# Sums of weight blocks on one engine, and gates' steps at another place, in a fused scan and router kernel

## The chip, the cores and the metric

The kernel runs on one core of a Trainium2 chip. The metric is device time in microseconds: the median of several executions on the same chip. Five engines work from queues of their own, each in order: TensorE (PE, with PEld for its weight loads), VectorE (DVE), ScalarE (ACT), GpSimd (POOL) and SyncE (SP, which here only starts transfers). They wait for each other through semaphores.

## The reference

Two parts follow each other. First a state-space scan over 4 batches, 8 heads and 768 positions gives 3072 rows of 256 numbers. Then a router with 8 experts picks one expert for each row by cosine similarity, and the row goes through that expert's two layers:

```python
xn = x / (np.linalg.norm(x, axis=-1, keepdims=True) + 1e-06)
logits = xn @ en.T / tau
expert_idx = np.argmax(logits, axis=1)
probs = softmax(logits)                      # written out in the reference
gate_w = probs[np.arange(N), expert_idx]
for e in range(E):
    mask = expert_idx == e
    h = np.maximum(x[mask] @ w1[e], 0.0)     # 256 -> 1024
    out[mask] = gate_w[mask, None] * (h @ w2[e])   # 1024 -> 256
```

Everything is float32. The change touches only the second part.

## The kernel before

The scan (`mamba`, `scan_end`) takes the first part of the span, and overlaps the first two experts. Its rows, with the router's logits beside them, go to DRAM. A table of row numbers by expert is built on the way. Then each expert is a `Job`: GpSimd gathers its rows (up to 416, four blocks of 104) with indirect DMAs (`load`, L876), PE turns them (`turn_x`, L970), the first layer gives hT (1024 hidden values by 416 rows), the second layer gives yT (256 by 416), PE turns that back (`out`, L1182), ACT scales it by the gate (L1185), and GpSimd scatters the rows to the output with an indirect DMA (L1188). What exceeds the 416 rows of an expert is handled after the experts in a loop (`leftover`) that runs over no block for this data; its small tables are made by the generator `leftover_blocks`, a few VectorE instructions at each `next(left)`.

Experts 0 and 1 are done in halves with plain products. For experts 2 to 7, the layers' products are made with seven block products in place of eight (Winograd's form of Strassen's method): each matrix is cut in 2 x 2 blocks, and sums and differences of blocks stand in for some blocks.

- `sum_w1(which, engine)` (L1019) makes four sums S1[0] to S1[3] of blocks of w1, each 128 x 512, at L1026. `sum_w2(n)` (L1028) makes one of four sums S of blocks of w2, also 128 x 512, at L1034. S1[1] uses S1[0], and S1[3] uses S1[1]; the same holds for S.
- `sum_x` (T1, 128 x 208 each) and `sum_h` (T, 128 x 832 each) make the four differences of the rows' side, on VectorE, at L1038.
- `up_blocks` (L1056) is the first layer as a generator of 14 blocks of two matmuls each. Blocks 0, 1 use a block of w1 alone and ACT copies their result as `p1` (L1081); 2, 3 lead to a sum into hT on VectorE (L1090) and a relu on ACT (L1086); 4, 5 use S1[1] and are copied as `u2`; 6, 7 use S1[0]; 8, 9 use S1[2], are copied as `u3` and lead to the next hT sums; 10, 11 add to the bank that `u3` was copied from; 12, 13 use S1[3] and add to the bank that the hT sums of 8, 9 read.
- `down_blocks` (L1131) is the second layer: seven products of four matmuls, with six VectorE sums of 128 x 208 (L1148, `u2`, `v`, `u3` and three into yT). It yields after the first and after the second product group, and then runs to its end.
- `Gates` (L1197) makes the gate of each row: `square` (ACT, L1209), `power` (GpSimd, L1215: the square root), `largest` (VectorE, L1222 and L1224), `scale` (VectorE, L1230 to L1232), `exp` (ACT, L1237), `end` (VectorE, L1242 to L1244).

PSUM banks rotate: four named `yp`, three `hp`, one `ot`. Weights have three buffers of each kind, and SP loads those of expert i + 3 at the end of expert i's second layer, held behind the gates' power. The order of all instructions on each engine is written by hand in `moe` (L1248): the code inside the loop over `j.up_blocks()` runs after each of its 14 blocks, and so do the steps between the parts of `down_blocks`. In `moe`, expert i's first layer carries, on GpSimd, the four sums of its w2 (after blocks 0, 2, 4 and 6), the four scatters of the expert before (blocks 1, 3, 5, 7), and, on VectorE, S1[2] and S1[3] (block 3) and the gates' steps (blocks 4 to 6) with leftover steps (5 to 7). Its second layer carries, on GpSimd, the gathers for an expert further on, S1[0] and S1[1] of the next expert, and the power.

Of the kernel before, what the change touches and what calls it, by code (L numbers as in the profile page):

```python
# [22 lines left out]
DM, E, F = NH * D, 8, 1024  # L23
# [47 lines left out]
def hold(k, dma, after):  # L71

    k.tc.add_manual_dep(
        dma.ins, after.ins.name, mybir.DependencyInfo(mybir.DependencyClass.Sync, mybir.DependencyReason.SCHED_ONLY),
        reason="behind other transfers",
    )


def load_weights(k, e, parts=(0, 1), after=None):
    nc = k.nc  # L80
    if 0 in parts:
        k.w1t[e] = k.wp.tile([128, KD, F], F32, name="w1", tag="w1")
        for v in range(2):
            d = nc.sync.dma_start(
                k.w1t[e][64 * v : 64 * v + 64], k.w1[e].rearrange("(v z p) f -> v p z f", v=2, z=KD)[v]
            )
            if after is not None:
                hold(k, d, after)
    if 1 in parts:
        k.w2t[e] = k.wp.tile([128, KF, DM], F32, name="w2", tag="w2")  # L90
        d = nc.sync.dma_start(k.w2t[e][:], k.w2[e].rearrange("(f p) m -> p f m", p=128))
        if after is not None and 0 not in parts:
            hold(k, d, after)
# [845 lines left out]
class Job:  # L939
# [76 lines left out]
            (S[2], a[0][0], a[1][0], ALU.subtract), (S[3], a[0][1], S[1], ALU.subtract),  # L1016
        )

    def sum_w1(s, which, engine):  # L1019
        if 0 in which:  # L1020
            s.S1 = s.tile([128, 4, F // 2], "S1", 1)
        a = [[s.w1[:, j, F // 2 * i : F // 2 * i + F // 2] for j in range(2)] for i in range(2)]
        sums = s.sums_of([s.S1[:, n] for n in range(4)], a)
        for n in which:
            out, x, y, op = sums[n]
            engine.tensor_tensor(out=out, in0=x, in1=y, op=op)  # L1026

    def sum_w2(s, n):  # L1028
        if n == 0:
            s.S = s.tile([128, 4, KF // 2, 128], "S", 1)  # L1030
        w = s.w2
        a = [[w[:, 4 * j : 4 * j + 4, 128 * i : 128 * i + 128] for j in range(2)] for i in range(2)]
        out, x, y, op = s.sums_of([s.S[:, n] for n in range(4)], a)[n]
        s.k.nc.gpsimd.tensor_tensor(out=out, in0=x, in1=y, op=op)  # L1034

    def sum_inputs(s, T, b):
        for n, x, y in ((0, b[0][1], b[0][0]), (1, b[1][1], T[0]), (2, b[1][1], b[0][1]), (3, b[1][0], T[1])):
# [93 lines left out]
    def down_blocks(s):  # L1131


        k, nc, m = s.k, s.k.nc, s.nt * s.tr // 2
        s.yT = s.tile([128, KD, 2 * m], "yoT")
        w = [[s.w2[:, 4 * j : 4 * j + 4, 128 * i : 128 * i + 128] for j in range(2)] for i in range(2)]

        def product(t, a, b, start=True):
            for f in range(4):
                nc.tensor.matmul(  # L1140
                    t, lhsT=a[:, f], rhs=b[:, f], start=start and f == 0, stop=(f == 3), skip_group_check=True
                )

        def bank():
            return s.bank("yp", 4)[:, 0:m]

        def add(out, x, y):
            nc.vector.tensor_tensor(out=out, in0=x, in1=y, op=ALU.add)  # L1148

        def part(name):  # L1150
            return s.tile([128, m], name, 1)[:]

        p1, u2, u3, v = (part(n) for n in ("q1", "v2", "v3", "v"))
        t1 = bank()
        product(t1, w[0][0], s.half(0, 0))
        nc.scalar.copy(out=p1, in_=t1)
        yield
        t3 = bank()
        product(t3, s.S[:, 3], s.half(1, 1))
        product(t1, w[0][1], s.half(1, 0), False)  # L1160
        nc.scalar.copy(out=s.yT[:, 0, 0:m], in_=t1)
        yield
        t6 = bank()
        product(t6, s.S[:, 1], s.T[:, 1])
        add(u2, t6, p1)
        add(v, t3, u2)
        t7 = bank()
        product(t7, s.S[:, 2], s.T[:, 2])
        add(u3, t7, u2)
        t4 = bank()  # L1170
        product(t4, w[1][1], s.T[:, 3])
        add(s.yT[:, 1, 0:m], t4, u3)
        t5 = bank()
        product(t5, s.S[:, 0], s.T[:, 0])
        add(s.yT[:, 0, m:], t5, v)
        add(s.yT[:, 1, m:], t5, u3)
# [71 lines left out]
def moe(k, second, late):  # L1248

    def begin(e):  # L1250
        j = Job(k, NT, TR, k.w1t[e], k.w2t[e])
        j.load(e)
        return j

    jobs = list(late)
    for j in [second] + jobs:
        j.bank_ = None
    last, e, left = second, 1, leftover_blocks(k)
    for i in range(2):
        j = jobs[i]  # L1260
        x = k.late_x if i == 0 else jobs[2].x
        gates = Gates(k, k.ep if i == 0 else k.p, x, TR, NT)
        for f in range(KF):
            j.up(f)
            if 1 <= f <= last.nt:
                last.out(f - 1)
            if f == 3:
                e += 1
                jobs.append(begin(e))
            if 3 <= f < 7:  # L1270
                gates.square(f - 3)
        gates.power()
        gates.largest()
        last, n = j, jobs[i + 1]
        n.turn_x()
        if i == 1:
            n.sum_w1((0, 1), k.nc.gpsimd)
        gates.scale()
        gates.exp()
        j.down(0)  # L1280
        g = gates.end()
        if i == 0:
            late[0].gate, late[1].gate = g[:, 0:HT], g[:, HT:]
        else:
            n.gate = g
        j.down(1)
        if i == 1:
            n.sum_x()
        load_weights(k, i + 3)
    gates = None  # L1290
    for i in range(2, E):
        j = jobs[i]
        for f, _ in enumerate(j.up_blocks()):
            if f < 8 and f % 2 == 0 and i < E - 1:
                j.sum_w2(f // 2)
            if f % 2 == 1 and f // 2 < last.nt:
                last.out(f // 2, True)
            if f == 3:
                j.sum_w1((2, 3), k.nc.vector)
            if gates is not None:  # L1300
                if f == 4:
                    gates.largest()
                    gates.scale()
                elif f == 5:
                    gates.exp()
                elif f == 6:
                    j.gate = gates.end()
            if i >= 3 and 5 <= f < 8:
                next(left, None)
        if i == E - 1:  # L1310
            k.nc.gpsimd.drain()
            return j
        last, n = j, jobs[i + 1]
        j.sum_h()
        if e + 1 < E:
            e += 1
            jobs.append(begin(e))
        n.sum_w1((0, 1), k.nc.gpsimd)
        gates = Gates(k, k.p, n.x, TR, NT)
        down = j.down_blocks()  # L1320
        next(down)
        n.turn_x(True)
        n.sum_x()
        next(down)
        for f in range(NT):
            gates.square(f)
        power = gates.power()
        for _ in down:
            pass
        if i + 3 < E:  # L1330
            load_weights(k, i + 3, after=power)
        if i == E - 2:
            for _ in left:
                pass
# [166 lines left out]
def kernel(  # L1501
# [37 lines left out]
    with (  # L1539
        tc.tile_pool(name="moe", bufs=2, reuse_waits="tile") as p,  # L1540
        tc.tile_pool(name="moe_ps", bufs=1, space=PSUM, reuse_waits="tile") as ps,
    ):
        k.p, k.ps = p, ps
        with tc.manual_schedule():
            last = moe(k, early[1], late)
        leftover(k)
        with tc.manual_schedule():
            moe_end(k, last)
# [43 lines left out]
```

## Time and profile before

Three executions took 279.1, 279.59 and 280.67 us, so the median is 279.59 us. The profiled execution itself took 280.93 us; its span, from the first to the last instruction, is 278.5 us.

| | busy us | share of span | instructions |
|---|---|---|---|
| PE | 250.3 | 90% | 2590 |
| DVE | 182.6 | 66% | 412 |
| ACT | 111.9 | 40% | 308 |
| POOL | 173.5 | 62% | 205 |

| group | count | mean us |
|---|---|---|
| L1026 DVE, sum of w1 blocks | 12 | 0.68 for one half of them, 1.94 median for the other |
| L1026 and L1034 POOL, sums of weight blocks | 32 | 1.28, six of them up to 1.96 |
| L1038 DVE, T 128x832 | 20 | 1.25 and 1.46 (two forms) |
| L1188 POOL, scatter | 32 | 1.09 |
| L876 POOL, gather | 32 | 1.19 |

How to read it: times are microseconds from the start of the span. In a timeline each line has its start, its length, the engine, the line of the kernel, the operation, output and inputs with their shapes, and in brackets the idle time before it with what ended it. Consecutive rows of one engine can overlap a little[...]; the distance between two starts is then what an instruction costs. A length includes time in which the instruction has started and stands still. PE's matmul ends are modelled. An entry x8 on PE is four logical matmuls in float32, and the granted clock is the share of full speed that PE was given.

### The profile page before, as it was taken

The page shows a single profiled execution, that of the slowest core. Times are in us where ns is not written, and L with a number is a line of the kernel's source. Part 1 is how long each engine was busy: PE and PEld are TensorE (multiplying, and loading weights), DVE is VectorE, ACT ScalarE, POOL GpSimd, SP SyncE. Part 2 cuts the span into 40 slices and gives each one's busy share as a digit, 9 for nine tenths or more (in the row PEclk, how much of TensorE's full clock was granted, in tenths as well). Part 3 has the DMA queues.
Part 4 walks back from the last instruction along what each step waited for, and adds up shares of the span by engine and source line. Part 5 has one row for each costly group of instructions (what it writes and reads, how often), then busy time and mean ns, then how long its engine had stood idle before and what let it go on. Part 6 is the DMA issues. An engine that isn't in the chain of part 4 may idle for free.

```text
span 278.5 us, 6675 instructions
## 1 busy us (share of the span) xinstructions
PE 250.3 (90%) x2590; PEld 230.2 (83%) x2590; DVE 182.6 (66%) x412; ACT 111.9 (40%) x308; POOL 173.5 (62%) x205
## 2 busy tenths in 40 slices
PE   7988999997999899997999699959977997999990
PEld 2676888886999799996999599859977996999990
DVE  6786888896744021449596987889497969846111
ACT  3614624521641223405644362553355353637300
POOL 8989466557126418487895886788387858416022
PEclk9999999999999999999999999998999999999997
DMA  4978584072899916987117623911482101002011
GB/s 132 301 231 264 176 253 148 30 198 62 225 271 244 244 44 146 257 188 209 30 47 165 186 65 84 255 48 44 107 227 58 32 15 39 3 0 55 9 29 32
DMA packets 22304, 35.89 MB, mean 129 GB/s; under 512 B 2547, under 2 KB 15550, under 8 KB 22272
## 3 DMA queue, kind: packets, MB, share of 16 engines
q1 hardware_dynamic: 19024, 28.73, 39.0%
q0 software_dynamic: 3072, 6.67, 8.9%
q8 instruction: 21, 0.34, 0.6%
q14 instruction: 11, 0.09, 0.1%
q10 hardware_dynamic: 176, 0.06, 0.1%
HBM read 29.05 MB, written 6.65 MB: 128 GB/s over the span
## 4 chain that ended last, share of the span: by engine, by line
PE 37%; DVE 23%; issue 15%; POOL 13%; DMA 8%; ACT 2%; POOLq 1%; DVEq 0%
PE yp L1140 12%; PE hp L1068 5%; DMA out_dram<-yo,to 4%; PE yp L1068 4%; DVE g L361 4%; DVE S L1026 4%; DMA xg<-y_rows,gi 4%; POOL xg L876 3%; DVE T L1038 3%; PE pg L351 2%; DVE gl L1224 2%; PE eb L983 2%; PE eb L1000 2%; POOL xb L278 2%; DVE gate L1243 2%
## 5 line engine op out<-in xcount | busy, mean ns | idle before, releaser
L1188 POOL DMA_INDIRECT out_dram<-yo,to x32 | 35.0, 1093 | 43.4 <-DVE yo L1187 26.2
L876 POOL DMA_INDIRECT xg<-y_rows,gi x32 | 38.1, 1190 | 16.3 <-issue 8.1
L1086 ACT ACTIVATE hT<-hT 128x416 f32<-128x416 f32 x36 | 19.6, 551 | 16.3 <-DVE hT L1090 14.4
L361 DVE TENSOR_TENSOR g<-pg,mask 128x1536 f32<-128x1536 f32 x12 | 21.1, 1755 | 5.9 <-PE pg L351 5.9
L1000 PE MATMUL yp<-hT,w 128*128 128x208 f32 x128 | 23.4, 340 | 0.3 <-PEq L1424 0.3
L1140 PE MATMUL yp<-T,S 128*128 128x208 f32 x120 | 23.0, 342 | 0.1
L1000 PEld LDWEIGHTS yp<-hT,w 128*128 128x128 f32 x128 | 22.3, 190 | 0.6 <-issue 0.6
L1140 PEld LDWEIGHTS yp<-T,S 128*128 128x128 f32 x120 | 21.0, 190 | 0.8 <-DVE v L1148 0.8
L1090 DVE TENSOR_TENSOR hT<-hp,u 128x416 f32<-128x416 f32 x24 | 13.8, 587 | 8.2 <-PE hp L1068 4.4
L1068 PE MATMUL yp<-T,S 128*128 128x208 f32 x96 | 18.9, 339 | 0.0
L1034 POOL TENSOR_TENSOR S<-w 128x512 f32<-128x512 f32 x10 | 12.8, 1285 | 9.0 <-PE yp L1140 8.9
L1140 PE MATMUL yp<-hT,w 128*128 128x208 f32 x80 | 17.1, 360 | 0.0
L1068 PEld LDWEIGHTS yp<-T,S 128*128 128x128 f32 x96 | 16.3, 190 | 0.0
L1068 PE MATMUL yp<-T,w 128*128 128x208 f32 x48 | 10.0, 352 | 6.2 <-ACT u L1081 6.2
L1140 PEld LDWEIGHTS yp<-hT,w 128*128 128x128 f32 x80 | 15.5, 205 | 0.1
L1081 ACT COPY p<-yp 128x416 f32<-128x416 f32 x12 | 6.0, 507 | 23.6 <-PE yp L1068 23.6
L1215 POOL TENSOR_TENSOR gr<-gr,half 104x4 f32<-104x4 f32 x8 | 9.6, 1201 | 9.0 <-ACT sq L1209 8.9
L1038 DVE TENSOR_TENSOR T<-hT,T 128x832 f32<-128x832 f32 x10 | 14.6, 1458 | 0.2
L1068 PEld LDWEIGHTS yp<-T,w 128*128 128x128 f32 x48 | 8.0, 189 | 8.0 <-ACT u L1081 7.9
L1038 DVE TENSOR_TENSOR T<-hT 128x832 f32<-128x832 f32 x10 | 12.5, 1252 | 3.1 <-ACT hT L1086 3.1
L1068 PE MATMUL hp<-xT,S 128*128 128x208 f32 x48 | 10.1, 354 | 4.4 <-DVE hT L1090 3.9
L1090 DVE TENSOR_TENSOR hT<-hp,p 128x416 f32<-128x416 f32 x12 | 7.1, 591 | 9.4 <-PE hp L1068 7.0
(247 smaller groups left out, 639.2 us busy)
## 6 DMA issues: line engine op xcount, KB each, us to landing
w<-in_moe_w_dram SPq DMA_DIRECT2D x16, 512.0 KB
w<-in_moe_w_dram SPq DMA_DIRECT2D x8, 1024.0 KB
y_rows<-rows SPq DMA_DIRECT2D x6, 528.0 KB
x<-in_x_dram SPq DMA_DIRECT2D x6, 512.0 KB
ct<-in_CT_dram SPq DMA_DIRECT2D x6, 256.0 KB
bi<-in_BT_dram SPq DMA_DIRECT2D x6, 256.0 KB
b<-in_B_dram SPq DMA_DIRECT2D x6, 256.0 KB
xa<-in_x_dram SPq DMA_DIRECT2D x6, 128.0 KB
```

The costliest lines, as they stand in the source:

```text
L361: t.masked = k.nc.vector.tensor_tensor(out=g[:], in0=k.pg[:, :, 0:384].rearrange("p q (u m) -> p q u m", u=2), in1=k.mask[:].unsqueeze(1). ...
L876: k.nc.gpsimd.indirect_dma_start(out=x, out_offset=None, in_=k.y_d[0:rows, :], in_offset=bass.IndirectOffsetOnAxis(ap=at, axis=0), bounds_ ...
L1000: nc.tensor.matmul(t, lhsT=s.w2[:, f, 128 * j : 128 * j + 128], rhs=s.hT[:, f, r], start=(f == 0), stop=(f == KF - 1))
L1026: engine.tensor_tensor(out=out, in0=x, in1=y, op=op)
L1034: s.k.nc.gpsimd.tensor_tensor(out=out, in0=x, in1=y, op=op)
L1038: s.k.nc.vector.tensor_tensor(out=T[n], in0=x, in1=y, op=ALU.subtract)
L1068: nc.tensor.matmul(t[:, m * u : m * u + m], lhsT=w[:, f : f + 128], rhs=x, start=start and u == 0, stop=True, skip_group_check=True,)
L1086: nc.scalar.activation(h, h, ACT.Relu)
L1090: nc.vector.tensor_tensor(out=h, in0=view(t), in1=view(p), op=ALU.add)
L1140: nc.tensor.matmul(t, lhsT=a[:, f], rhs=b[:, f], start=start and f == 0, stop=(f == 3), skip_group_check=True)
L1188: d = nc.gpsimd.indirect_dma_start(out=k.out[:, :], out_offset=bass.IndirectOffsetOnAxis(ap=s.to[:, i : i + 1], axis=0), in_=y[:], in_offs ...
L1215: return s.k.nc.gpsimd.tensor_tensor(out=s.r[:], in0=s.r[:], in1=s.k.half[0 : s.tr, 0 : s.nt], op=ALU.pow)
```

## The change

All sums of weight blocks are made on VectorE. `sum_w1` of the next expert is no longer split between GpSimd (in the second layer) and VectorE (in the first layer, block 3): all four are made in the second layer, one after each of the last four products of `down_blocks`, which gets three more `yield`s for it. For expert 2 they stand behind the second plain layer and `sum_x`. The four `sum_w2` stand together at block 3 of the first layer. The gates' `largest` and `scale` and three leftover steps move from blocks 4 to 7 of the first layer to the end of the second layer before it; `exp` moves from block 5 to block 0, and `end` from block 6 to block 3. On GpSimd, experts 2 to 7 leave only gathers, scatters and the power. The order of instructions on PE and on SP is the same before and after.

```diff
@@ sum_w1, sum_w2
-    def sum_w1(s, which, engine):
+    def sum_w1(s, which):
...
-            engine.tensor_tensor(out=out, in0=x, in1=y, op=op)
+            s.k.nc.vector.tensor_tensor(out=out, in0=x, in1=y, op=op)
...
-        s.k.nc.gpsimd.tensor_tensor(out=out, in0=x, in1=y, op=op)
+        s.k.nc.vector.tensor_tensor(out=out, in0=x, in1=y, op=op)
@@ down_blocks
         add(v, t3, u2)
+        yield
...
         add(u3, t7, u2)
+        yield
...
         add(s.yT[:, 1, 0:m], t4, u3)
+        yield
@@ moe, experts 0 and 1
-        if i == 1:
-            n.sum_w1((0, 1), k.nc.gpsimd)
         gates.scale()
...
         if i == 1:
             n.sum_x()
+            n.sum_w1(range(4))
@@ moe, experts 2 to 7
         for f, _ in enumerate(j.up_blocks()):
-            if f < 8 and f % 2 == 0 and i < E - 1:
-                j.sum_w2(f // 2)
             if f % 2 == 1 and f // 2 < last.nt:
                 last.out(f // 2, True)
-            if f == 3:
-                j.sum_w1((2, 3), k.nc.vector)
-            if gates is not None:
-                if f == 4:
-                    gates.largest()
-                    gates.scale()
-                elif f == 5:
-                    gates.exp()
-                elif f == 6:
+            if f == 0 and gates is not None:
+                gates.exp()
+            elif f == 3:
+                if gates is not None:
                     j.gate = gates.end()
-            if i >= 3 and 5 <= f < 8:
-                next(left, None)
+                if i < E - 1:
+                    for h in range(4):
+                        j.sum_w2(h)
...
-        n.sum_w1((0, 1), k.nc.gpsimd)
...
         power = gates.power()
-        for _ in down:
-            pass
+        for h in range(4):
+            next(down, None)
+            n.sum_w1((h,))
+        gates.largest()
+        gates.scale()
+        for _ in range(3):
+            next(left, None)
```

## The prediction

> **What bounds the kernel now.** I read the busy table first (PE 250.3 us of 278.5, no other engine above 66%), then the chain of waits. Up to about 123 us no instruction changes its place. From there the experts 2 to 7 run, each as an up stage (first layer, 14 blocks) and a down stage (second layer). Cutting the span at PE's first matmul of each gives the table by stage; its columns are PE, PEld, DVE, ACT and POOL busy, granted clock, DMA share, GB/s. Up and down stages alternate (experts 3, 4, 5, 6, then the up stage of 7):
>
> ```profile
> 148.10:161.60 13.50, 11.28 (x66) 10.46 (x66) 10.38 (x23) 6.96 (x17) 10.68 (x10) 1.00 0.70 183
> 161.60:172.50 10.90, 10.85 (x66) 10.49 (x65) 9.50 (x14) 4.50 (x15) 8.19 (x6) 1.00 0.22 55
> 172.50:187.40 14.90, 11.51 (x66) 10.67 (x66) 11.62 (x23) 7.21 (x18) 11.90 (x10) 0.98 0.64 166
> 187.40:199.40 12.00, 12.00 (x65) 11.82 (x64) 9.29 (x13) 4.24 (x15) 7.50 (x5) 0.88 0.16 38
> 199.40:213.60 14.20, 11.26 (x65) 10.44 (x65) 11.26 (x24) 6.95 (x17) 11.39 (x10) 1.00 0.66 171
> 224.40:237.60 13.20, 11.21 (x65) 10.39 (x65) 10.38 (x21) 6.92 (x17) 9.50 (x8) 1.00 0.11 30
> 248.20:259.10 10.90, 10.90 (x66) 10.31 (x64) 5.98 (x17) 7.61 (x17) 4.60 (x4) 1.00 0.14 40
> ```
>
> Down stages are PE from end to end. Up stages are not, except the last: with the same matmuls and POOL busy 4.6 us instead of 10 to 12, it takes 10.9. The long down stage of expert 4 (12.00, all PE busy) has a granted clock of 0.88; I don't count it as a wait. In PE's timeline the gap stands at two blocks:
>
> ```profile
> 157.73 1.67 PE L1068 MATMUL yp<-T,w 128*128 128x208 f32 x8 [1.54 <-ACT u L1081]
> 160.08 1.67 PE L1068 MATMUL hp<-xT,S 128*128 128x208 f32 x8 [0.68 <-DVE hT L1090]
> ...
> 256.20 1.67 PE L1068 MATMUL yp<-T,w 128*128 128x208 f32 x8
> 257.71 1.57 PE L1068 MATMUL hp<-xT,S 128*128 128x208 f32 x8
> ```
>
> The first two are expert 3, the last two expert 7. ACT's copy `u` is late because ACT, in order, waits for the gates' exp, and that for VectorE's gate steps. VectorE is late for this reason (expert 4, then 7):
>
> ```profile
> 176.31 1.94 DVE L1026 TENSOR_TENSOR S<-w 128x512 f32<-128x512 f32 x1
> 178.17 0.68 DVE L1026 TENSOR_TENSOR S<-w,S 128x512 f32<-128x512 f32 x1
> 178.98 1.54 DVE L1224 TENSOR_TENSOR gl<-xg,gm 104x32 f32<-104x32 f32 x1
> 181.55 1.47 DVE L1243 TENSOR_SCALAR gate<-gate 104x4 f32<-104x4 f32 x1
> ...
> 252.04 0.68 DVE L1026 TENSOR_TENSOR S<-w 128x512 f32<-128x512 f32 x1
> 252.64 0.69 DVE L1026 TENSOR_TENSOR S<-w,S 128x512 f32<-128x512 f32 x1
> 253.46 0.19 DVE L1224 TENSOR_TENSOR gl<-xg,gm 104x32 f32<-104x32 f32 x1
> 254.69 0.17 DVE L1243 TENSOR_SCALAR gate<-gate 104x4 f32<-104x4 f32 x1
> ```
>
> GpSimd's timeline (POOL) in the same places:
>
> ```profile
> 176.41 1.28 POOL L1034 TENSOR_TENSOR S<-S,w 128x512 f32<-128x512 f32 x1
> ...
> 179.18 1.29 POOL L1034 TENSOR_TENSOR S<-w 128x512 f32<-128x512 f32 x1
> ...
> 181.69 1.29 POOL L1034 TENSOR_TENSOR S<-w,S 128x512 f32<-128x512 f32 x1
> ...
> 252.68 1.54 POOL L1188 DMA_INDIRECT out_dram<-yo,to  x1 [0.58 <-ACT yo L1185]
> ```
>
> Each slow VectorE row lies on a GpSimd sum and ends with it; the same rows beside a scatter (252.68) cost nothing extra. So in the up stage GpSimd's sums delay VectorE by 1.26 + 1.35 + 1.30 = 3.9 us.
>
> **The change part by part.** The order of PE's and SP's instructions stays as it is; what moves is on VectorE, ACT and GpSimd.
>
> Removed: 32 GpSimd sums of about 1.28 us (two `sum_w1` for each of experts 2 to 7, four `sum_w2` for each of 2 to 6). Added to VectorE: the same sums, which join the 12 that it has. Their issue distance there is 252.64 - 252.04 = 0.60 us, so four `sum_w2` at block 3 of up cost 2.4 us and four `sum_w1` in down 2.4 us, where two (1.2 us) stood in up. VectorE's load per expert is then six hT sums 3.7, four T 3.85, four xT differences 1.2, six sums of products 1.9, sums of weights 4.8, gates 1.45, leftover steps 0.6 to 2.1: about 18 us in a 21.5 us period. It fits; its order decides.
>
> Up stage, counted from PE's first matmul. Down's last two VectorE sums end at 0.86 (148.97 - 148.11), the fourth `sum_w1` at 1.46, gates' `largest` and `scale` at 2.38 (253.24 to 254.16 is 0.92). ACT's exp, now after the first copy `p1`, ends at 2.65 and the second `p1` at 3.1; its reader, the second hT sum, was ready at 3.25 anyway. Then the leftover steps on VectorE, ahead of the first hT sum that was ready at 2.6: 0.9 us in expert 3, 2.0 in expert 4 (183.15 to 185.00 and `begin`), 2.1 in expert 5, 0.6 in expert 6. So that sum starts at 3.3, 4.4, 4.5, 3.0. Behind it stand the second (0.6), gates' end (0.5) and `sum_w2` (2.4): free at 7.4, 8.5, 8.6, 7.1. The next hT sum waits for ACT's third copy, at 7.95 at the earliest (256.18 - 248.23), so `sum_w2` lies in the cover of PE's blocks 4 to 8; without that cover it would cost its 2.4 us. What is queued behind the late hT sum is ACT's relu, then `yo`, `u`, relu, `u`, `yo`, `yo`, `u`. In experts 3 and 6 that chain still meets PE's blocks 8 to 10. In 4 and 5 it reaches the copy that block 10 waits for at about 8.6 instead of 7.9: a new wait of 0.7 and 0.85 us, 1.55 together (bounds: nothing if ACT catches up, 2 x 1.8 if the whole lateness passes through).
> Before, the up stages lasted 13.48 (148.11 to 161.59), 14.88, 14.20 and 13.25, together 55.8. After: 4 x 10.9 + 1.55 = 45.15. **Gain 10.65.**
>
> Down stage: T and xT differences end 6.45 us after its start, the first sum of products is ready at 6.55, and the `sum_w1` steps (0.60) fall between products 1.41 us apart. The power, 1.1 us on GpSimd, falls there; if it blocks one step for its whole length, product banks are still read in time. Down stages are PE-bound already (10.72, 10.91, 10.78, 10.59, and 12.03 at the low clock). Taking 10.7 and leaving the clock dip as it is: **gain 0.2**, bounds -0.5 and +1.5.
>
> Expert 2's up stage: the gates' rows `gr` 1.24 and `gl` 1.11 at 124.08 shrink to 0.16 and 0.19, so the column copy `yoT` ends at 125.8 instead of 128.3, and the transposes that wait 0.78 and 0.87 us go at once. But all four `sum_w1` now stand before the hT sums: xT differences end at 127.0, `sum_w1` at 129.4, hT 130.05 and 130.65, about where they were (129.54 to 130.8). PE's blocks 8 and 9 then wait on ACT's copies, to 132.6; down starts at 136.2 instead of 137.39. **Gain 1.2** (0 to 1.8).
>
> GpSimd keeps, per expert, four scatters, four gathers and the power, none later than now; SP's weight loads, held by the power, go up to 1 us earlier and are needed two experts later. Tail and start: nothing.
>
> Here a page speaks against the change. The Trainium skill (SBUF — State Buffer, "SBUF: two separate sides") says that the port pair which the two engines share is locked for a whole instruction, and its box on software descriptors that a VectorE operation on both ports keeps GpSimd from writing them: about 620 ns alone, 3100 overlapped. It names single-input copies for that, yet the rows show it for two-input sums too, smaller: 1.54 at 252.68 and 1.92 at 188.89 (a gather beside T), against 1.02 to 1.08. By the row, eight transfers with 0.5 to 0.8 more are 8 x 1.9 + 8 x 0.3 + 1.1 = 19 us of GpSimd at worst, within 21.5. By the page's 3.1 us it is 28.3, and GpSimd would set the period. I take the row.
>
> Sum: 10.65 + 0.2 + 1.2 = 12.05. The profiled execution took 280.93 (span 278.5 and 2.4 around it), 1.3 over the median of 279.59; it becomes 268.9, the median 267.5.
>
> **Rivals.** (a) VectorE's order becomes the bound: `sum_w2` and leftover steps hold the hT sums, so that every up stage loses about 1.5 us more at blocks 10 to 12. For it: 18 us of 21.5 in a fixed order. Against: the stage of expert 7 carries 3.0 us in the same place (two sums and all gate steps) and still idles 1.11 before the hT sum. 4 x 1.5: 273.5.
> (b) A denser PE is granted less clock: one dip such as expert 4's (1.3 us) in each of five experts instead of one. For it: that row; against: the dense stage of expert 7 at 1.00. 4 x 1.3: 272.7.
> (c) Slower: the starved descriptors above. At 28.3 us per expert against 25.0 now (148.11 to 248.23 over four), five experts lose 16 us: 296. It decides once a transfer costs 1.15 us more than alone (8 x 1.4 + 1.1 + 9.2 = 21.5). No row shows more than 0.85.
> (d) The change doesn't do what it says: the gates' delay goes, but the wait passes whole to something the trace of before doesn't show: 279.6.
>
> **How the numbers follow.** Forecast 0.66 (264.5 to 270.5), (a) 0.14, (b) 0.08, (c) 0.06, (d) 0.03, better than 264.5 0.03. The range 264.5 to 273.5 takes in the forecast, most of (b) and half of (a). Within 0.5% is about what a measurement can tell from no change: faster 0.91, same 0.03, slower 0.06.
>
> **What would show it.** Right: no VectorE sum of weights above 0.7 us except beside the power; up stages at 10.9 to 11.7; exp on ACT before the second `p1`; small waits at block 10 in experts 4 and 5 only. Wrong: idle time of PE's `hp<-xT,S` put down to hT sums (a), granted clock below 0.95 in several stages (b), scatters and gathers above 2.2 us (c).

## The result and the profile after

The changed kernel takes 266.32 us (median of 4 runs, 265.75 to 266.91), against 279.35 us for the kernel before (4 runs, 278.6 to 280.67). The ratio is 0.9529, 95% interval 0.9487 to 0.9571: 13.0 us less. The forecast was 267.5, from 264.5 to 273.5. The profiled execution of the changed kernel took 266.37 us, with a span of 264.6.

The table by stage of the changed kernel, cut as before at PE's first matmul of each stage. The columns are the stretch, its length, busy time of PE, PEld, DVE, ACT and POOL, granted clock, DMA share and GB/s. The rows are the up stage of expert 3, up and down of 4, and up of 6:

```profile
147.89:158.78 10.89, 10.89 (x66) 10.44 (x66) 8.57 (x26) 7.38 (x17) 5.72 (x6) 1.00 0.82 205
...
169.36:180.53 11.17, 11.01 (x66) 10.44 (x66) 9.35 (x26) 7.08 (x17) 5.29 (x5) 1.00 0.79 197
180.53:191.11 10.58, 10.58 (x65) 10.55 (x65) 9.02 (x17) 4.28 (x14) 5.56 (x5) 1.00 0.22 66
...
212.89:223.78 10.89, 10.89 (x66) 10.44 (x66) 8.15 (x24) 7.41 (x17) 4.56 (x4) 1.00 0.13 36
```

The up stages of experts 3 and 6 are now as short as that of expert 7 was before, PE from end to end; that of 4 is 0.28 longer, and so is that of 5 (11.19). POOL is busy 4.6 to 5.7 us in them, where it was 9.5 to 11.9. In these four up stages VectorE makes four sums in place of two and is busy for less, 8.2 to 9.4 us where it was 10.4 to 11.6. Over the whole span it has 32 instructions more and is busy 173.0 us in place of 182.6. The added sums are about 21 us of work (32 x 0.66), so by this estimate some 31 us of the old 182.6 were instructions that had started and stood still.

PE's timeline of the changed kernel at the places where it waited (the first two rows are expert 2, then block 10 and 12 of expert 3, then block 10 of expert 4):

```profile
129.30 1.67 PE L1068 MATMUL yp<-T,S 128*128 128x208 f32 x8 [0.19 <-DVE S L1026]
...
132.68 1.82 PE L1068 MATMUL yp<-T,S 128*128 128x208 f32 x8 [0.29 <-ACT u L1081]
...
155.86 1.67 PE L1068 MATMUL yp<-T,w 128*128 128x208 f32 x8
157.37 1.57 PE L1068 MATMUL hp<-xT,S 128*128 128x208 f32 x8
...
177.61 1.67 PE L1068 MATMUL yp<-T,w 128*128 128x208 f32 x8 [0.17 <-issue]
```

The waits of 1.54 and 0.68 us in expert 3 are gone. What is left is 0.17 at block 10 in experts 4 and 5, and two small waits in expert 2.

VectorE's timeline of the changed kernel from the end of expert 3's down stage into the up stage of expert 4 (169.36 on):

```profile
168.45 0.68 DVE L1026 TENSOR_TENSOR S<-w 128x512 f32<-128x512 f32 x1
...
170.95 0.19 DVE L1227 TENSOR_TENSOR gl<-xg,gm 104x32 f32<-104x32 f32 x1
...
174.86 0.17 DVE L1246 TENSOR_SCALAR gate<-gate 104x4 f32<-104x4 f32 x1
...
175.16 0.66 DVE L1034 TENSOR_TENSOR S<-w 128x512 f32<-128x512 f32 x1
```

The three rows that took 1.94, 1.54 and 1.47 us before (the w1 sum S1[2], `gl`, `gate`) take 0.68, 0.19 and 0.17. The last row shown is the first of the four w2 sums.

GpSimd's timeline of the changed kernel in the same stage:

```profile
177.09 1.53 POOL L1191 DMA_INDIRECT out_dram<-yo,to  x1 [0.38 <-ACT yo L1188]
178.93 0.99 POOL L1191 DMA_INDIRECT out_dram<-yo,to  x1 [0.31 <-ACT hT L1086]
```

The scatter at 177.09 starts with the last VectorE sum (177.07) and takes half a microsecond more than the next one, which lies beside none. That is the price that was feared in its large form. The longest transfer of experts 2 to 7 is a gather of 1.85 us (161.37), beside a `T` row of 128x832.

### The profile page after: what moved, and what is told of

It reads as the page before. It is cut to its first block, busy times and chain, and to the rows that moved or that the text cites. A ratio compares the mean times of both kernels' runs of the same rounds, so it can differ in the third digit from the quotient of the medians.

```text
span 264.6 us, 6644 instructions
## 1 busy us (share of the span) xinstructions
PE 247.8 (94%) x2589; PEld 230.1 (87%) x2590; DVE 173.0 (65%) x444; ACT 112.0 (42%) x308; POOL 127.9 (48%) x173
## 4 chain that ended last, share of the span: by engine, by line
PE 49%; issue 19%; POOL 18%; DVE 7%; DMA 4%; POOLq 1%; ACT 1%; DVEq 0%
PE yp L1140 15%; PE yp L1068 9%; PE hp L1068 6%; PE eb L983 4%; DMA out_dram<-yo,to 4%; PE eb L1000 4%; POOL xb L278 4%; POOL xg L876 3%; DVE g L361 3%; POOL out_dram L1191 2%; POOL xs L265 2%; POOL spread L110 1%; PE pz L613 1%; PE yp L970 1%; PE hp L983 1%
## 5 line engine op out<-in xcount | busy, mean ns | idle before, releaser
L876 POOL DMA_INDIRECT xg<-y_rows,gi x32 | 36.7, 1148 | 15.5 <-issue 7.9
L1000 PE MATMUL yp<-hT,w 128*128 128x208 f32 x128 | 23.4, 340 | 0.3 <-PEq L1424 0.3
L1000 PEld LDWEIGHTS yp<-hT,w 128*128 128x128 f32 x128 | 22.3, 190 | 0.6 <-issue 0.6
L1140 PE MATMUL yp<-hT,w 128*128 128x208 f32 x80 | 15.7, 339 | 0.0
L1140 PEld LDWEIGHTS yp<-hT,w 128*128 128x128 f32 x80 | 14.2, 190 | 0.0
L413 ACT COPY yT<-py 128x512 f32<-128x512 f32 x12 | 6.4, 589 | 15.7 <-PE py L402 15.7
L1212 ACT ACTIVATE sq<-xg 104x256 f32<-104x256 f32 x32 | 12.9, 408 | 0.0
L983 PE MATMUL eb<-xT,w 128*128 128x208 f32 x64 | 12.8, 345 | 0.0
L1081 ACT COPY u<-yp 128x416 f32<-128x416 f32 x24 | 12.0, 505 | 1.9 <-PE yp L1068 1.6
L983 PE MATMUL hp<-xT,w 128*128 128x208 f32 x64 | 12.2, 339 | 0.0
L1038 DVE TENSOR_TENSOR T<-hT 128x832 f32<-128x832 f32 x10 | 10.2, 1020 | 3.1 <-ACT hT L1086 2.5
L544 POOL TENSOR_TENSOR pre<-pre,ob 128x8 bf16<-128x8 bf16 x24 | 4.8, 199 | 15.3 <-DVE ob L539 13.8
```

What stands on the lines that cost most here:

```text
L876: k.nc.gpsimd.indirect_dma_start(out=x, out_offset=None, in_=k.y_d[0:rows, :], in_offset=bass.IndirectOffsetOnAxis(ap=at, axis=0), bounds_ ...
L983: nc.tensor.matmul(t, lhsT=s.w1[:, j, 128 * f : 128 * f + 128], rhs=s.xT[:, j, :], start=(j == 0), stop=(j == KD - 1))
L1000: nc.tensor.matmul(t, lhsT=s.w2[:, f, 128 * j : 128 * j + 128], rhs=s.hT[:, f, r], start=(f == 0), stop=(f == KF - 1))
L1081: nc.scalar.copy(out=p[:], in_=t[:, 0 : 2 * m])
L1140: nc.tensor.matmul(t, lhsT=a[:, f], rhs=b[:, f], start=start and f == 0, stop=(f == 3), skip_group_check=True)
L1212: s.k.nc.scalar.activation(sq[:], s.x[:, i, :].rearrange("p (j w) -> p j w", j=KD)[:, :, 0:128], ACT.Square, accum_out=s.r[:, i : i + 1],)
```

## The experiments

Ten runs. Each is timed against the kernel before on the same chip; diffs are against the changed kernel. The stage lengths come from PE's timeline of each profiled execution; the down column is the sum of the five down stages (experts 2 to 6). "Start" is the time of expert 2's first matmul, which the change doesn't touch. The kernel before had a median of 278.47 us beside runs 1, 2, 3 and 5, of 279.5 beside 4 and 8, and of 280.58 beside 6, 7, 9 and 10. So whole times are compared between rows by their ratios; 0.01 is about 2.8 us.

| kernel | median us | ratio [95%] | start | up 2 | up 3 | up 4 | up 5 | up 6 | down |
|---|---|---|---|---|---|---|---|---|---|
| before | 279.35 | 1 | 124.88 | 12.51 | 13.48 | 14.88 | 14.20 | 13.25 | 55.03 |
| changed | 266.32 | 0.9529 [0.9487, 0.9571] | 125.70 | 11.60 | 10.89 | 11.17 | 11.19 | 10.89 | 52.92 |
| 1 gates alone | 272.71 | 0.9779 [0.9697, 0.9861] | 124.33 | 12.51 | 10.99 | 12.11 | 14.92 | 10.98 | 54.80 |
| 2 sums alone | 267.31 | 0.9612 [0.9549, 0.9676] | 124.16 | 11.60 | 11.26 | 12.07 | 11.78 | 11.25 | 52.93 |
| 3 spare GpSimd sums | 280.28 | 1.0054 [1.0013, 1.0096] | 124.07 | 15.67 | 13.21 | 13.39 | 14.74 | 12.94 | 52.92 |
| 4 spare GpSimd fills | 270.66 | 0.9690 [0.9571, 0.9808] | 124.00 | 13.20 | 11.36 | 12.16 | 14.21 | 11.36 | 52.93 |
| 5 half of w1's sums back | 266.51 | 0.9578 [0.9514, 0.9641] | 123.85 | 11.61 | 10.89 | 11.16 | 11.19 | 10.89 | 55.00 |
| 6 one more VectorE sum | 265.98 | 0.9488 [0.9435, 0.9541] | 127.80 | 11.60 | 10.89 | 11.16 | 11.19 | 10.89 | 52.93 |
| 7 three more | 271.82 | 0.9710 [0.9652, 0.9768] | 127.18 | 12.41 | 11.54 | 12.51 | 12.54 | 11.07 | 52.94 |
| 8 two VectorE copies | 266.81 | 0.9552 [0.9431, 0.9673] | 123.62 | 11.69 | 11.00 | 11.84 | 12.07 | 10.89 | 52.91 |
| 9 leftover steps later | 264.97 | 0.9459 [0.9412, 0.9506] | 126.57 | 10.91 | 10.89 | 10.89 | 10.89 | 10.89 | 52.92 |
| 10 changed, again | 265.91 | 0.9499 [0.9458, 0.9540] | 124.68 | 11.63 | 10.89 | 11.17 | 11.20 | 10.89 | 52.92 |

The theory: GpSimd's sums hold VectorE's rows, these make the gates and hT sums late, and PE waits at blocks 10 and 12. The first rival: the places of the gates' steps are what counts, and who makes the sums matters little. The second: GpSimd had too much work, and anything taken from it would have helped.

**1. The gates' and leftover steps moved, the sums where they were.**

```diff
-    s.k.nc.vector.tensor_tensor(out=out, in0=x, in1=y, op=op)
+    s.k.nc.gpsimd.tensor_tensor(out=out, in0=x, in1=y, op=op)
...
+    if f < 8 and f % 2 == 0 and i < E - 1:
+        j.sum_w2(f // 2)
...
+    if f == 3:
+        j.sum_w1((2, 3), k.nc.vector)
...
+    n.sum_w1((0, 1), k.nc.gpsimd)
```

> Half of the change: gates' steps and leftover steps at their new places, all sums of weight blocks as before (GpSimd's sums in both layers, two on VectorE at block 3). Theory (GpSimd's sums hold VectorE up, wherever the gate steps stand): the 3.9 us of delay in each up stage stay and only fall on other VectorE rows (the second-layer sums, gate steps at other places); part is hidden since ACT's exp no longer stands before the copies of blocks 8 and 9. Up stages 12 to 13 us, total about 272 (270 to 275). Rival (the placement of the gates is what was worth it): up stages 10.9 to 11.2 and a total of 266 to 267.

Measured: 272.71 us (270.29 to 273.31), between the two kernels as expected. The way there was not: up stages of 12 to 13 us were expected throughout, and experts 3 and 6 came to 10.99 and 10.98. VectorE's rows stand still as before (a sum of 2.45 in expert 3), but `exp` is already done, so the lateness stays in the cover of PE's blocks. In expert 5 it doesn't. VectorE's row there, GpSimd's beside it, and PE's wait:

```profile
196.56 2.07 DVE L1405 TENSOR_SCALAR left_b<-left_b 128x28 f32<-128x28 f32 x1
```

```profile
197.32 1.27 POOL L1034 TENSOR_TENSOR S<-S,w 128x512 f32<-128x512 f32 x1
```

```profile
199.41 0.97 PE L1068 MATMUL hp<-T,S 128*128 128x208 f32 x4 [1.83 <-DVE hT L1090]
```

A row of 28 elements a partition starts at 196.56 and ends with GpSimd's sum, at 198.6; the hT sum behind it starts at 198.78, and PE waits 1.83 us. This stage also had a granted clock of 0.89, which makes its 14.92 longer than the wait alone; in stretches of 2 us, the clock is 0.50 from 202 to 204, soon after this wait.

**2. The sums on VectorE, the gates' and leftover steps at their old places.**

```diff
-    if f == 0 and gates is not None:
-        gates.exp()
...
+    if gates is not None:
+        if f == 4:
+            gates.largest()
+            gates.scale()
+        elif f == 5:
+            gates.exp()
+        elif f == 6:
             j.gate = gates.end()
+    if i >= 3 and 5 <= f < 8:
+        next(left, None)
```

> The other half: all sums of weight blocks on VectorE as in the change, gates' steps and leftover steps at their old places (blocks 4 to 7 of the first layer), behind the four sums of w2. Theory: VectorE rows are short (no row of gates or sums above 0.7 us), most of the gain is there; exp comes later, at about 7.2 us of the up stage, so block 10 waits 0.4 and block 12 up to 0.6 in experts 4 and 5: 268.5 (267 to 270). Rival (placement is what counts): 274 to 279.

Measured: 267.31 us (267.06 to 267.85). The sums are the main part. By the table's up stages against before, the sums alone are worth 10.36 us (0.91 + 2.22 + 2.81 + 2.42 + 2.00) and the whole change 12.58, so the gates' new places add 2.2. Alone, the gates' move is worth 6.8 (0 + 2.49 + 2.77 - 0.72 + 2.27). (The -0.72 has the clock dip of run 1 in it.) The parts add up to more than the whole, since each of them breaks the same chain. What the old places still cost, in PE's timeline in expert 4:

```profile
178.74 1.67 PE L1068 MATMUL hp<-xT,S 128*128 128x208 f32 x8 [0.55 <-DVE hT L1090]
```

On VectorE the last leftover step starts at 177.80, directly ahead of the hT sums (178.11) that block 12 waits for.

**3. The changed kernel, and GpSimd makes the four sums once more in each up stage, into a tile Z that nobody reads.**

```diff
+    def spare(s, n):
+        if n == 0:
+            s.Z = s.tile([128, 4, KF // 2, 128], "Z", 1)
...
+        out, x, y, op = s.sums_of([s.Z[:, n] for n in range(4)], a)[n]
+        s.k.nc.gpsimd.tensor_tensor(out=out, in0=x, in1=y, op=op)
...
+    if f < 8 and f % 2 == 0 and i < E - 1:
+        j.spare(f // 2)
```

> The changed kernel, with four sums of w2 blocks made once more on GpSimd in each up stage of experts 2 to 6, at the places of before, into a tile that nobody reads (extra work, no new waits for other engines). Theory (the engines exclude each other): each spare sum holds VectorE for up to 1.28 us; 3.9 to 5.1 us per up stage, of which VectorE's slack before the hT sums of block 8 hides 0.5 in experts 3 and 6: about 3 us in each of five up stages, so 279 to 284. GpSimd rows 1.28 us, some stretched. Rival (the gain came from GpSimd's own queue being shorter or from the place of the gates): only scatters and gathers come later, total within 1 us of 266.3.

Measured: 280.28 us (277.31 to 281.28), at a clock of 1.00 in these stages. Nothing waits for Z, and yet the whole gain is gone: the five up stages are 14.2 us longer than in the changed kernel. VectorE's row, GpSimd's beside it, PE's wait, in expert 4:

```profile
182.71 2.13 DVE L1034 TENSOR_TENSOR S<-w 128x512 f32<-128x512 f32 x1
```

```profile
182.99 1.29 POOL L1042 TENSOR_TENSOR Z<-w 128x512 f32<-128x512 f32 x1
```

```profile
186.00 1.67 PE L1076 MATMUL hp<-xT,S 128*128 128x208 f32 x8 [1.04 <-DVE hT L1098]
```

VectorE's sum starts first, ends 0.56 us after GpSimd's, and takes 1.45 more than its neighbours (0.68). So it is the running beside each other that costs, not a result that comes late.

**4. The same with fills: four memsets of 128x2048 on GpSimd in each up stage.** They are longer than a sum and read nothing.

```diff
+    def spare(s, n):
...
+        s.k.nc.gpsimd.memset(s.Z[:], float(n))
```

> The changed kernel with four GpSimd fills (memset, 128 x 2048) in each up stage of experts 2 to 6, where the spare sums of e3 stood: GpSimd is busy there as well, but reads no tensor. Theory: what holds VectorE is GpSimd's reading of two tensors, so VectorE's rows of weights and gates stay at 0.68 and 0.17 to 0.2 us beside a fill, and the up stages of experts 3 to 6 stay at 10.9 to 11.2: total 266 to 267. Rival (any GpSimd instruction with SBUF operands holds VectorE): rows stretched as in e3, up stages 13 or more, 276 to 283.

Measured: 270.66 us (two runs, 270.03 and 271.28). Both expectations failed: not free, and not the price of the sums. The five up stages are 6.6 us longer than in the changed kernel. VectorE's timeline (three rows of expert 4, one of 5), then GpSimd's, then PE's:

```profile
175.64 0.18 DVE L1250 TENSOR_REDUCE gate<-gl 104x4 f32<-104x32 f32 x1
175.85 1.25 DVE L1251 TENSOR_SCALAR gate<-gate 104x4 f32<-104x4 f32 x1
...
179.13 0.69 DVE L1034 TENSOR_TENSOR S<-w,S 128x512 f32<-128x512 f32 x1
...
197.07 2.59 DVE L1410 TENSOR_SCALAR left_b<-left_b 128x28 f32<-128x28 f32 x1
```

```profile
175.25 1.82 POOL L1039 MEMSET Z<- 128x2048 f32 x1
...
178.78 1.83 POOL L1039 MEMSET Z<- 128x2048 f32 x1
...
197.80 1.82 POOL L1039 MEMSET Z<- 128x2048 f32 x1
```

```profile
200.44 0.97 PE L1073 MATMUL hp<-T,S 128*128 128x208 f32 x4 [2.22 <-DVE hT L1095]
```

The sum at 179.13 lies wholly beside a fill and keeps its 0.69, and the TENSOR_REDUCE at 175.64 keeps its 0.18. But the TENSOR_SCALAR rows, of 4 and 28 elements a partition, end with the fill (175.25 + 1.82 = 177.07; 175.85 + 1.25 = 177.10), and the one at 197.07 costs PE 2.22 us. So there are two cases: a two-input row is held by a GpSimd operation that reads, and a TENSOR_SCALAR row by one that only writes as well. The Trainium skill (SBUF — State Buffer, "SBUF: two separate sides") has the same two cases: VectorE takes the shared pair of ports when it runs in a two-port mode, or with two SBUF inputs, and the latter "only against a GpSimd op that reads SBUF". It also says that whoever starts first has the pair for the whole instruction. The recorded starts do not show that: the held rows of run 3 and of 197.07 begin 0.28 and 0.73 us ahead of GpSimd's sum and fill. But a scatter, begun earlier, was still running on GpSimd both times, so which operation had the pair first is not settled. That the TENSOR_SCALAR rows run in such a mode is inferred from this, not measured.

Run 4 also bears on the second rival. Each fill takes GpSimd longer than a spare sum (1.82 against 1.29), yet the fills cost less than half as much, so it is not the length of GpSimd's work that counts.

**5. The changed kernel, with the first two of the next expert's w1 sums back on GpSimd in the down stage.**

```diff
+        n.sum_w1((0, 1), k.nc.gpsimd)
...
         for h in range(4):
             next(down, None)
-            n.sum_w1((h,))
+            if h >= 2:
+                n.sum_w1((h,))
```

> The changed kernel, with the first two sums of w1 of experts 3 to 7 back on GpSimd in the second layer, the other two on VectorE in the second layer. Theory (only GpSimd sums in the up stage cost, since the down stage has cover): VectorE's T rows are stretched to about 2 us again, PE doesn't wait; down stages 10.6 to 10.9, total 266.5 to 267.5. Rival (every GpSimd sum costs its length): 5 x 2.5 us, 277 to 279.

Measured: 266.51 us (266.23 to 266.92). VectorE's row and GpSimd's in the down stage of expert 3:

```profile
162.68 2.29 DVE L1038 TENSOR_TENSOR T<-hT,T 128x832 f32<-128x832 f32 x1
```

```profile
162.81 1.27 POOL L1026 TENSOR_TENSOR S<-w 128x512 f32<-128x512 f32 x1
```

A `T` row of 1.02 takes 2.29. The up stages stay as in the changed kernel, and the five down stages lose 2.1 us. Of this 1.4 is in the first, where a `T` row ends at 141.6 and PE waits 1.17 at 141.75; no wait had been expected there, and 10.6 to 10.9 in place of its 11.99. By the ratios, run 5 is 1.4 us slower than the changed kernel and 2.2 slower than run 10, though the intervals overlap. The spans of the profiles differ less, in part because the start is 1.85 us earlier here than in the changed kernel's profile; against run 10, with a start 0.83 later, the span is 1.1 longer. The sums of the up stage carry most of the gain; those of the down stage are worth about 2 us in the stages, and the whole times don't fix it more closely.

**6 and 7. The changed kernel, with one or three more VectorE sums of 0.6 us behind the four at block 3.** They test the rival that VectorE's order is the next bound.

```diff
             for h in range(4):
                 j.sum_w2(h)
+            j.spare(1)
```

> The changed kernel with one more sum of w2 blocks (0.60 us) on VectorE behind the four at block 3, in experts 2 to 6, into a tile that nobody reads. Theory (the place is covered by PE's blocks 4 to 11): VectorE is ready for the hT sum of block 8 up to 0.6 us late, PE's block 12 asks for it 0.7 us later still: no cost, 266.3 to 266.8. Rival (VectorE's order is already the bound): 5 x 0.6 = 3 us, 269.3.

> The same with three more sums (1.8 us) in each of the five up stages. Theory: hT sums of block 8 end 0.35 (expert 3), 1.0 (4), 1.0 (5), 0 (6) and 0.6 us (2) after PE asks for them at block 12: 3 us, 269.3 (268.5 to 270.5). Rival (no cover): 5 x 1.8 = 9 us, 275. Rival (far more cover): 266.3.

Measured: 265.98 us with one (265.08 to 268.53) and 271.82 with three (271.3 to 273.15; 269.3 had been expected). With one, every stage is as long as without. With three, VectorE's row of the three and then PE's wait in expert 4:

```profile
180.61 2.14 DVE L1039 TENSOR_TENSOR Z<-w 128x512 f32<-128x512 f32 x3
```

```profile
183.31 1.67 PE L1075 MATMUL hp<-xT,S 128*128 128x208 f32 x8 [1.07 <-DVE hT L1097]
```

1.8 us of work made PE wait 1.07 here, so about 0.7 was free. All five up stages lose 4.3 (0.81 + 0.65 + 1.34 + 1.35 + 0.18); 3.0 were expected. The room is not the same everywhere: the waits are as long in expert 5 (1.08), shorter in 2 and 3 (0.53 and 0.39), and absent in 6. The rest of the distance to the changed kernel in this profile is the start, 127.18.

**8. The changed kernel, with two VectorE copies of 128x1024 from SBUF to SBUF behind the four sums.** They test the starved descriptors of the slower rival, with the operation that the page names.

```diff
+    for n in range(2):
+        s.k.nc.vector.tensor_copy(out=s.Z[:], in_=s.w2[:, 4 * n : 4 * n + 4, :])
```

> The changed kernel with two VectorE copies of 128 x 1024 from SBUF to SBUF behind the four sums of w2 at block 3 of experts 2 to 6, beside GpSimd's scatters: a test of the third rival of the prediction (starved descriptors). Rival: scatters beside the copies grow to 3 us, GpSimd's scatters and gathers run late. Theory: a scatter waits at most for the VectorE instruction it meets, so 1.5 to 2.2 us, and GpSimd's slack (it is busy 10 of 21.5 us) takes it; the copies cost 0.6 to 1.1 us each on VectorE, about 1.2 to 2.2 us in the place where e6_dve_plus3 put 1.8: total 267 to 271.

Measured: 266.81 us (two runs, 266.09 and 267.52), just under what was expected. VectorE's rows in expert 4, then GpSimd's there and, last, one of expert 2:

```profile
175.18 0.68 DVE L1034 TENSOR_TENSOR S<-w,S 128x512 f32<-128x512 f32 x1
175.78 1.47 DVE L1039 COPY Z<-w 128x1024 f32<-128x1024 f32 x2
```

```profile
175.21 1.53 POOL L1196 DMA_INDIRECT out_dram<-yo,to  x1 [0.38 <-ACT yo L1193]
177.04 1.07 POOL L1196 DMA_INDIRECT out_dram<-yo,to  x1 [0.30 <-issue]
```

```profile
131.91 1.59 POOL L876 DMA_INDIRECT xg<-y_rows,gi  x1 [0.31 <-PE yp L1073]
```

The scatter of 1.53 us starts with the last sum, as in the changed kernel without copies, so that length is not the copies' doing; it is not longer for the copies that follow, and the next scatter takes 1.07. The clean case is the gather: it begins 0.09 us after the copies of expert 2 (131.82) and takes 1.59, where the same gather takes 1.11 in the changed kernel (133.98). The copies cost 0.67 in expert 4 (11.84 against 11.17), which is their 1.4 less the 0.7 that is free by run 7. No scatter or gather comes near 3 us; the longest takes 1.89, beside a `T` row.

**9. The leftover steps behind blocks 9 to 11, and expert 2's S1[2] and S1[3] behind its first hT sums; 10. the changed kernel once more beside it.**

```diff
-            n.sum_w1(range(4))
+            n.sum_w1((0, 1))
...
+                if i == 2:
+                    j.sum_w1((2, 3))
...
+            if i < E - 1 and f in (9, 10, 11):
+                next(left, None)
...
-        for _ in range(3):
-            next(left, None)
```

> The changed kernel with the leftover steps moved behind blocks 9 to 11 of the first layer (behind VectorE's hT sums of blocks 8 and 9), and expert 2's third and fourth sum of w1 behind its first two hT sums. Theory (the only waits left between 125 and 245 us are 0.28 and 0.30 us in experts 4 and 5 from the leftover steps, and 0.71 in expert 2 from four sums of w1 ahead of the hT sums): all up stages at 10.9, up to 1.3 us less than the changed kernel, about 265.2 (264.8 to 265.8). Rival (these waits come from ACT's or GpSimd's side): no change, 266.3.

> The changed kernel once more, beside the others on the same chip, for a direct comparison: 266.3, within 0.3%.

Measured: 264.97 us (263.69 to 266.55, 6 runs) against 265.91 (265.26 to 266.59, 6 runs). PE's timeline of run 9, block 10 of expert 4:

```profile
177.51 1.67 PE L1068 MATMUL yp<-T,w 128*128 128x208 f32 x8
```

The wait of 0.17 is gone, there and in expert 5, and so is that of 0.29 in expert 2; all up stages last 10.89 to 10.91. From expert 2's start to the end of expert 7's first layer that is 1.3 us less (118.74 against 120.05). The medians differ by 0.94 and the intervals overlap, so the gain is shown in the stages and not settled in the whole time. It is the lowest median of all kernels here.

## Why the prediction was right, point by point

**The mechanism was right.** That GpSimd's sums hold VectorE, and that this makes PE wait, is shown by run 3: unread sums alone bring the whole time back. Run 2 answers the first rival, since most of the gain comes with the gates at their old places, and run 4 the second. The mechanism was told too narrowly, though, as "each slow VectorE row lies on a GpSimd sum": run 4 shows that fills hold TENSOR_SCALAR rows too. The changed kernel has neither in these stages.

**Up stages of experts 3 to 6: 10.65 predicted, 11.67 measured** (55.81 to 44.14). Experts 3 and 6 are at 10.89 as said. The new waits were placed rightly (block 10, experts 4 and 5 alone) and sized too large: 0.7 and 0.85, against 0.28 and 0.30 in stage length. The late hT sum was nearly right (4.3 us after the start of expert 4's stage; 4.4 had been said). The term that was most off is ACT's queue behind it. From that sum's start to block 10 it had been given 4.2 us; in the trace it is 3.95 (173.66 to 177.61), ACT's operations in that queue following each other about 0.4 us apart. The rest is that 0.1, and that block 10 comes at 7.97 even where nothing holds it (expert 3), in place of 7.9. Run 9 confirms the cause: with the leftover steps out of the way, both waits vanish.

**Down stages: 0.2 predicted, 2.11 measured**, which is beyond the upper bound of 1.5. The long one of expert 4 (12.03, clock 0.88) is 10.58 at a clock of 1.00 in the changed kernel. That is 1.45, a dip that the forecast left as it was. In stretches of 2 us, it is a clock of 0.73, 0.50 and 0.92 from 186 to 192. It begins soon after PE's waits of 1.53 and 1.85 us at blocks 10 and 12, as the dip of run 1 follows a wait of 1.83. The eight profiles in which PE never waits more than 1.2 us in these stages have no such dip there. So the change may have taken the dip away with the waits; but waits of 1.99 in run 3 and 2.22 in run 4 have no dip behind them, and the cause stays open. The other 0.66 are small waits of before which the forecast of 10.7 for each left in.

**Expert 2: 1.2 predicted, 0.91 measured.** The two waits of 0.19 and 0.29 in the timeline above are those of S1 ahead of block 4 and of ACT's copy at block 8; the second had been foreseen, the first not.

**The start: nothing predicted, 0.82 lost.** The scan is the same, and expert 2 begins at 125.70 in one profile of the changed kernel and at 124.68 in the other. In the first, the stretch from 69 to 80 us has a granted clock of 0.84 (1.00 in that of before). The starts of all twelve profiles run from 123.6 to 127.8.

**The sum.** 12.05 was predicted. The two profiled executions differ by 14.56 (280.93 to 266.37), and the terms account for it: 11.67 + 2.11 + 0.91 - 0.82 is 13.87 in the span, and 0.7 lies outside it. The medians differ by 13.0. The median is missed by 1.2 us, the profiled execution by 2.5; the profile of before carried the clock dip of 1.45, and whether the other executions of before had one is not on record. That the median came so near is in part luck: in the profiles, the later start hides most of what the up stages gave beyond the forecast.

**The rivals.** (a) VectorE's order as the next bound is not what happened: block 12 waits nowhere in the changed kernel. Run 7 shows how near it is: about 0.7 us of VectorE work is free in the up stages of experts 4 and 5 and more in the others, and past that PE waits. (b) The denser PE keeps its clock: it is 1.00 in every stage from expert 2 to the first layer of expert 7, as in the four rows above. (c) The slower rival needed 1.15 us more for each transfer. The longest scatter and gather here took 1.53 and 1.85, 0.5 and 0.8 more than alone, as the row of before had said; run 8 with the kind of copy that the page warns of gave 1.59. The Trainium skill's 3.1 us (the page and section named above) is not seen in any run. Its rule that the wait lasts until VectorE's instruction ends, given there for a copy, fits that gather and the scatter at 177.09: the sum beside the scatter ends at 177.75, so 0.66 us of it was left, and the scatter took 0.5 more. With instructions of 0.7 us there is little to wait for; a much longer one was not tried. (d) is refuted by the time itself.

## What to carry to other kernels

Before an operation is given to an idle engine, look whether the engine's work makes other rows longer: here a sum of 1.28 us on GpSimd cost the VectorE rows shown beside it 1.26 to 1.90 us each, while VectorE makes the same sum in 0.60. A row that is long for its size, and ends with a row of another engine, is the sign. When two edits break the same chain, their gains do not add, so each is to be tried alone before the sum is believed; and how much an engine has to spare in a stage is measured by adding work to it in small steps.

## What was not expected of the hardware

A GpSimd fill of 128x2048 (1.82 us) leaves two-input VectorE sums at 0.69 us, yet holds a TENSOR_SCALAR of 104x4 or 128x28 until it ends (1.25 and 2.59 us in place of 0.17 and 0.18). So a small step can be the more exposed one; but not every small step is, as the TENSOR_REDUCE of 104x32 beside the same fill kept its 0.18. VectorE rows with an operand in PSUM (the hT sums, 0.5 us each) were not seen longer beside any GpSimd sum or fill. And the granted clock dips at places that change from run to run. The three dips above read as 0.84 to 0.89 over 11 to 15 us, but in stretches of 2 us each is a fall to 0.50 that is over within 6 us, worth 1 to 2 us, which is as much as the differences that runs 5, 9 and 10 were to settle.
